# Chunk 1's attention output from channel-major products, with a repeated denominator divided on VectorE

## The chip, the cores and the metric

The kernel runs on one NeuronCore of a Trainium2 chip. The core has five engines with instruction streams of their own: TensorE (PE in the profile, with its weight loads as PEld), VectorE (DVE), ScalarE (ACT), GpSimd (POOL) and SyncE (SP, which issues most transfers). The metric is the device time of one execution in microseconds; lower is better.

## The reference

Two blocks follow one another. Everything is float32 at the kernel's inputs but `w_in`, `w_out`, `S1` and `S2`, which arrive as float64 and are rounded to float32 on the chip.

```python
# attention: batch 4, heads 4, seq 1088, head_dim 32, r = 8 sketches
a, b = S1 @ x, S2 @ x              # per token, 8 values each
phi(x) = outer(a, b)               # 64 features per token and head
kv  = sum_s phi(k)[s,f] * v[s,d]   # 64 x 32 per head
z   = sum_s phi(k)[s,f]            # 64 per head
x   = (phi(q) @ kv) / (phi(q) @ z + 1e-6)      # numerators / denominator

# MLP: 4352 tokens, d_model 128, d_ff 2048
h = x @ w_in
out = (0.5 * h * (1 + erf(h / sqrt(2)))) @ w_out
```

## The kernel before

**Tiling.** 1024 of a batch's 1088 tokens are cut into two chunks of 512 tokens, so there are eight chunks (0 to 7), and one of the 64-token remainders. For the MLP a chunk needs x in the form [128 channels, 512 tokens]; the 128 channels are 4 heads by 32. `w_in` and `w_out` lie in five pieces of 256, 256, 512, 512 and 512 columns (or rows) of d_ff; they are numbered 0 to 4 here. A piece is 128 columns times fi, so that fi 0 and 1 lie in piece 0, fi 2 and 3 in piece 1, fi 4 to 7 in piece 2.

**The MLP's steps.** `hidden(n, fi)` (L734) multiplies x of chunk n with 128 columns of `w_in` into one of two PSUM banks (`h_ps`), and ScalarE takes the GELU of it (L747). With two banks, a `hidden` waits until the GELU of the one before the last has emptied its bank. `first_hidden(n, half)` (L749) is the product for fi = 0, issued by halves of 256 tokens. `project(n, fi)` (L914, in the profile L925) multiplies a GELU output with the rows of `w_out` at fi. This usual way serves fi 0 to 3 of chunk 0 and fi 0 to 7 of chunk 1. All later blocks of four fi go by a method with seven half-size products in place of eight: GpSimd forms `token_sums` of the GELU outputs (L783, in the profile L791 to L794), and `two_products` (L813, L826) issues the products in pairs, two 64-column tiles side by side. The sums of `w_out` that this needs, `channel_sums(i)` of piece i (L768, L778 to L781), are formed once, on GpSimd too.

**The main loop** (L1256) goes through steps t. Steps 0 to 3 are chunk 0 with fi 0 to 3, steps 4 to 11 chunk 1 with fi 0 to 7, then chunk 0 goes on with fi 4 to 15, and so on. In each step come `hidden`, then the extra work that `at(t, ...)` put there, then the products that are due. Two steps are written out by hand, t = 3 and t = 4 (L1272, L1286). At its end the kernel fixes the order of the text on each engine: no engine's instructions are reordered, so an instruction that waits holds up all that stand behind it on its engine.

**Rounding the weights.** Each piece, two 32-bit words per weight, takes a chain: two field extractions on VectorE (L283 `bits_e`, L288 `bits_a`), the low word (L270) and the exponent (L294 `bits_r`, which needs L283) on ScalarE, then mantissa (L302 `bits_m`), sign (L307) and product (L312). Pieces 0 and 1 are done ahead of step 4. Pieces 2 to 4 are the six `turns`, from `begin(turns[0])` in step 4 on, nearly one after the other on VectorE. ScalarE's part of `turns[0]` is issued in step 4 ahead of the GELU of chunk 1's first hidden product.

**Chunk 1's x before the change** (step 3). `numerators_by_token` (L678, L685) has TensorE multiply the query features (64 features of two heads on 128 partitions, `qp`) with `kz_apart`, which holds kv and z side by side, so that numerators and denominators come out as [token, head x 33]. `divide` (L691) adds 1e-6, takes the reciprocal and multiplies on VectorE (L696, L698, L700), and `turn_half` (L717, L721) transposes the result by halves on TensorE into [channel, token]; ScalarE copies one half out of PSUM (L722) and VectorE the other. In between stand the rounding of `w_out` piece 1, whose mantissa step is done by ScalarE and GpSimd (L299, L300), and `project(0, 0)` and `project(0, 1)`, the latter in two halves between the transposes.

**z for chunk 0 and 1.** `z_cols` holds batch 0's z, each value repeated over 2 x 32 columns. Before the change it is made at step 40 (L525) and used at one place, `turn_first_kv` (L528).

**After piece 4.** In steps 13 to 16 `key_turn_blocks(1, r)` transposes batch 1's keys on VectorE (L383) and `features_of_all(1)` has TensorE use them (L1043). GpSimd makes piece 4's `w_out` product (`multiply`, L1141), and then goes on with `channel_sums(2)` and the first `token_sums`.

Of the kernel before, what the change touches and what calls it, by code (L numbers as in the profile page):

```python
# [8 lines left out]
FP = mybir.dt.float32  # L9
U32 = mybir.dt.uint32  # L10
AX = mybir.AluOpType
# [5 lines left out]
def kernel(  # L17
# [18 lines left out]
    pe, dve, act, pool, sp = nc.tensor, nc.vector, nc.scalar, nc.gpsimd, nc.sync  # L36
    B, H, S, D = q.shape
    R = S1.shape[0]
    F = R * R
# [3 lines left out]
    NP = H // 2  # L43
# [3 lines left out]
    JC = 4  # L47
    CW = JC * 128
    G = 128 // 32
    NCH = J // JC  # L50
    C = D + 1
# [9 lines left out]
    big = ctx.enter_context(tc.tile_pool(name="big", bufs=1))  # L61
    att = ctx.enter_context(tc.tile_pool(name="att", bufs=2))
# [9 lines left out]
    def work_bank():  # L72
        return work_banks()[:, 0]

    def halves(banks):
        return [banks[:, i] for i in range(2)]
# [437 lines left out]
        dve.tensor_mul(out=S_abc[b][:, :, :, 4:8], in0=c.rearrange("p (i f) -> p i f", i=2)[:, :, None].broadcast_to([128, 2, 2, 4]),  # L514
                       in1=own_r[:, None, :, None].broadcast_to([128, 2, 2, 4]))

    def repeat_first_z():

        to = kz_first.rearrange("f (c r d) -> f c r d", c=NP, r=2)
        for c in range(NP):  # L520
            act.copy(out=to[:F, c], in_=kz_apart[c * F:(c + 1) * F, :, c, 0:D])
        zs = att.tile([128, 2, D], FP, name="z_cols")
        for c in range(NP):
            rows = slice(c * F, (c + 1) * F)
            pool.tensor_copy(out=zs[rows], in_=kz_apart[rows, :, c, D:C].broadcast_to([F, 2, D]))  # L525
        held["zs"] = zs

    def turn_first_kv():  # L528

        ps, zs = work_bank(), held["zs"]  # L530
        for c in range(NP):
            pe.matmul(ps[c * F:(c + 1) * F, :F], lhsT=zs.rearrange("f r d -> f (r d)"), rhs=ident[:, c * F:(c + 1) * F],
                      start=True, stop=True)
        sketch_of_z(0, ps, 0)

# [128 lines left out]
    def take_x(n):  # L664

        W, banks, m = width[n], numerators_in.pop(n), 1 if n < NMAIN else B // 2
        xT[n] = att.tile([128, CW], FP, name="xT", bufs=3)
        to = xT[n][:, :W]
        to = to.rearrange("p (s x) -> p s x", s=2) if m == 1 else to.rearrange("p (s t i) -> p s i t", s=2, i=m)
        act.copy(out=to, in_=banks[:, :, :W // 2] if m == 1 else banks[:, :, :W // 2].rearrange("p s (i t) -> p s i t", i=m))  # L670

    x_tok = {}

# [4 lines left out]
    def numerators_by_token(n, banks, tokens):  # L678

        for at, i in enumerate(tokens):  # L680
            to = by_head(banks[at // 2]).rearrange("p (j c r) x -> p j r c x", j=2, c=NP)[:, at % 2]
            for r in range(2):
                for half in range(2):
                    rows, tok = slice(half * 64, (half + 1) * 64), i * 128 + half * 64
                    pe.matmul(to[rows, r], lhsT=qp[n][:, r, tok:tok + 64], rhs=kz_apart[:, r], start=True, stop=True)  # L685
# [5 lines left out]
    def divide(n, banks, first, den=None):  # L691

        if den is None:
            den = att.tile([128, NP, 2 * H], FP, name="den_tok")
            for i, bank in enumerate(banks):
                dve.tensor_scalar(out=den[:, i], in0=by_head(bank)[:, :, D], scalar1=1e-6, scalar2=None, op0=AX.add)  # L696
        den = den[:, :len(banks)]
        dve.reciprocal(out=den, in_=den)  # L698
        for i, bank in enumerate(banks):
            dve.tensor_mul(out=x_half(n, first + i).rearrange("p j h d -> p (j h) d"), in0=by_head(bank)[:, :, 0:D],  # L700
                           in1=den[:, i, :, None].broadcast_to([128, 2 * H, D]))
# [15 lines left out]
    def turn_half(n, i, ps, copy):  # L717
        if i == 0:
            xT[n] = att.tile([128, CW], FP, name="xT", bufs=3)
        for j in range(2):  # L720
            pe.transpose(ps[:, j * 128:(j + 1) * 128], in_=x_tok[n, i][:, j].rearrange("p h d -> p (h d)"), identity=ident)  # L721
        copy(out=xT[n][:, i * 256:(i + 1) * 256], in_=ps[:, :256])  # L722
# [26 lines left out]
    def first_hidden(n, half):  # L749

        if half == 0:
            first_banks[n, 0] = hidden_bank()
        parts = 1 if n else 2
        for i in range(parts):
            cols = slice(half * 256 + i * 256 // parts, half * 256 + (i + 1) * 256 // parts)
            pe.matmul(first_banks[n, 0][:, cols], lhsT=w_tile(w_in_sb, 0), rhs=xT[n][:, cols], start=True, stop=True)  # L756
# [157 lines left out]
    def project(n, fi, parts=range(B // 2), cols=slice(None)):  # L914
        first, final = fi == (BLOCKED if n == NMAIN else 0), fi == (USUAL[n] if n < NCH else NF) - 1
        if first and n not in o_of:
            o_of[n] = out_bank() if n < NMAIN else [out_bank() for i in range(B // 2)]
        g = g_of[n, fi]
        if n == NMAIN:

            for i in parts:
                pe.matmul(o_of[n][i][:, :128], lhsT=g[:, i * 128:(i + 1) * 128], rhs=w_tile(w_out_sb, fi),  # L922
                          start=first, stop=final)
            return
        pe.matmul(o_of[n][:, cols], lhsT=w_tile(w_out_sb, fi), rhs=g[:, cols], start=first, stop=final)  # L925
# [72 lines left out]
    for c in range(NP):  # L998
        rows = slice(c * F, (c + 1) * F)
        act.copy(out=kz_apart[rows, :, c], in_=kv_bank[rows, :128].rearrange("f (r x) -> f r x", r=2)[:, :, :C])  # L1000
    w_in[0].exponents()
    w_in[0].mantissas()
    by_act(**late.pop())
# [29 lines left out]
    def at(t, f, *a):  # L1033
        slots[t].append(lambda: f(*a))
# [40 lines left out]
    held = {}  # L1075
# [55 lines left out]
        for f in what:  # L1131
            getattr(rounding[w.name], f)()

    def end(w, product_by):
        r = rounding[w.name]
        r.mantissas()
        r.signs()
        if product_by is dve:
            r.product()

    def multiply(w):  # L1141
        rounding[w.name].product(pool)

    turns = [w[i] for i in range(2, 5) for w in (w_in_sb, w_out_sb)]
    both, low, exp = ("low_words", "exponents"), ("low_words",), ("exponents",)
# [1 line left out]
    for k, acts in enumerate(schedule):  # L1147
        t1 = acts[-1][0] if acts else 4
        if k + 1 < len(turns):
            at(t1, begin, turns[k + 1])  # L1150
        for t, what in acts:
            at(t, by_scalar, turns[k], *what)
        at(t1, end, turns[k], dve if k < 5 else pool)
    at(12, widen_v_rem, 1)
    at(13, multiply, turns[5])
    for i, t in enumerate((5, 6, 14)):
        at(t, channel_sums, i)
    at(16, channel_sums, 3)
    for r in range(2):
# [14 lines left out]
    at(26, lambda: turn_kv(1, held["kv"]))  # L1174
    at(24, query_outer, 2)
    at(6, spread_sketches)
    at(40, repeat_first_z)
    for n in range(3, NCHUNK):

        t = (n - 1) * NF  # L1180
# [75 lines left out]
    for t in range(len(steps) + LAG):  # L1256
        if t < 4:

            hidden(0, t)
            if t == 0:  # L1260
                expand_multiply(1, 0)
                w_out[0].fields()
                expand_copy(1, 1)
                expand_multiply(1, 1)
            if t == 1:
                w_out[0].low_words()
                w_out[0].exponents()
                w_out[0].finish()
                w_out[1].fields()
            if t == 2:  # L1270
                w_out[1].low_words()
            if t == 3:  # L1272
                banks = work_banks()
                numerators_by_token(1, halves(banks), range(JC))
                w_out[1].mantissas(by_pool=True)
                w_out[1].exponents()
                divide(1, halves(banks), 0)
                w_out[1].signs()
                w_out[1].product()
                project(0, 0)  # L1280
                project(0, 1, cols=slice(0, 256))
                turn_half(1, 0, work_bank(), by_act)
                project(0, 1, cols=slice(256, 512))
                turn_half(1, 1, work_bank(), by_dve)
            continue
        if t == 4:  # L1286
            begin(turns[0])
            by_scalar(turns[0], *both)
            first_hidden(1, 0)
            for f, *a in products[t]:  # L1290
                f(*a)
            first_hidden(1, 1)
        for n in drains[t]:
            drain(n)
        sooner = t == NMAIN * NF
        if sooner:
            for f, *a in products[t]:
                f(*a)
        if t < len(steps):
            n, fi = steps[t]  # L1300
            hidden(n, fi, by_halves=t >= 18)
        if t < len(steps) and steps[t][0] < NMAIN and steps[t][1] % NB == NB - 1:
            n, b = steps[t][0], steps[t][1] // NB
            if b >= first_block(n):
                token_sums(n, b)
        for f in slots[t]:
            f()
        for n in done[t]:
            store(n)
        if t != 4 and not sooner:  # L1310
            for f, *a in products[t]:
                f(*a)
    for n in done[len(steps) + LAG]:
# [40 lines left out]
```

## Time and profile before

| | us |
|---|---|
| median of 3 runs | 258.32 (257.75 to 258.34) |
| the profiled execution, its own time | 257.65 |
| its span | 255.9 |
| TensorE busy | 251.8 (98%) |
| VectorE busy | 156.9 (61%) |
| ScalarE busy | 114.6 (45%) |
| GpSimd busy | 177.6 (69%) |

A float32 product appears as two records on TensorE, one per pass: 512 columns through the whole array take 0.43 us each, 256 columns 0.215 us. The duration of a record contains the way through the array; what counts for the throughput is the distance from one start to the next. In a row of the timeline, "x4" joins four records, and the second number is the time from the first start to the last end. An instruction on VectorE, ScalarE or GpSimd that follows another without a wait starts a little before the other's recorded end.

### The profile page before, as it was taken

How to read it: one execution, taken by the hardware profiler on the slowest of the kernel's cores; microseconds unless marked ns; L12 is line 12 of the kernel's file. 1: busy time of each engine (PE TensorE's matmuls, PEld its weight loads, DVE VectorE, ACT ScalarE, POOL GpSimd, SP SyncE). 2: the span in 40 equal slices, each digit the busy share in tenths (PEclk: the TensorE clock that was granted, in tenths of full speed). 3: DMA queues.
4: the chain of work that ended last, by engine and by line, in shares of the span. 5: the costliest groups of instructions: out<-in, count | busy, mean ns of one | idle time of the engine just before them, and what ended most of it. 6: DMA issues, size and time to landing. Idle time of an engine off the chain costs nothing.

```text
span 255.9 us, 5994 instructions
## 1 busy us (share of the span) xinstructions
PE 251.8 (98%) x2427; PEld 132.7 (52%) x2427; DVE 156.9 (61%) x331; ACT 114.6 (45%) x221; POOL 177.6 (69%) x194
## 2 busy tenths in 40 slices
PE   8999999999999999999999999999999999999995
PEld 4755444555454546454444455445544444445784
DVE  4899995929798996570278976399507000700382
ACT  3785885323535334533335332623444334433541
POOL 3419329998849776687758874787758777877950
PEclk9999999999999999999999999999999999999999
DMA  6689657810001101111000011000110200020021
GB/s 210 205 267 295 168 116 195 222 31 10 0 3 18 23 4 23 20 19 25 3 0 0 0 17 29 1 4 0 27 16 7 36 1 3 5 36 3 0 35 31
DMA packets 29083, 13.50 MB, mean 53 GB/s; under 512 B 21888, under 2 KB 27264, under 8 KB 29056
## 3 DMA queue, kind: packets, MB, share of 16 engines
q1 hardware_dynamic: 28624, 12.79, 20.5%
q8 instruction: 19, 0.31, 0.5%
q10 hardware_dynamic: 432, 0.33, 0.4%
q14 instruction: 8, 0.07, 0.1%
HBM read 10.88 MB, written 2.23 MB: 51 GB/s over the span
## 4 chain that ended last, share of the span: by engine, by line
PE 98%; ACT 0%; DVE 0%; issue 0%
PE h_ps L740 45%; PE o_ps L826 35%; PE o_ps L925 4%; PE w_ps L896 2%; PE w_ps L456 1%; PE w_ps L604 1%; PE w_ps L659 1%; PE w_ps L957 1%; PE w_ps L570 1%; PE o_ps L922 1%; PE h_ps L756 1%; PE o_ps L445 1%; PE w_ps L1043 1%; PE h_ps L348 1%; PE w_ps L685 0%; PE o_ps L397 0%
## 5 line engine op out<-in xcount | busy, mean ns | idle before, releaser
L740 PE MATMUL h_ps<-xT,w_in 128*64 128x512 f32 (+2 forms) x536 | 138.0, 567 | 0.0
L747 ACT ACTIVATE block<-h_ps 128x512 f32<-128x512 f32 (+1 forms) x132 | 75.4, 572 | 119.5 <-PE h_ps L740 117.6
L826 PE MATMUL o_ps<-block,w_out 128*64 128x256 f32 x232 | 59.5, 379 | 0.0
L791 POOL TENSOR_TENSOR bits_low<-block 128x512 f32<-128x512 f32 x29 | 37.2, 1281 | 28.4 <-ACT block L747 28.4
L740 PEld LDWEIGHTS h_ps<-xT,w_in 128*64 128x64 f32 (+1 forms) x536 | 41.4, 140 | 26.9 <-issue 8.4
L826 PEld LDWEIGHTS o_ps<-block,w_out 128*64 128x64 f32 x232 | 31.7, 137 | 38.6 <-issue 27.4
L792 POOL TENSOR_TENSOR bits_a<-block 128x512 f32<-128x512 f32 x29 | 37.0, 1276 | 12.6 <-ACT block L747 12.6
L841 DVE COPY sums<-o_ps 64x256 f32<-64x256 f32 x8 | 3.3, 417 | 58.9 <-PE o_ps L826 58.9
L793 POOL TENSOR_TENSOR bits_e<-bits_a,block 128x512 f32<-128x512 f32 x29 | 37.3, 1288 | 2.3
L794 POOL TENSOR_TENSOR bits_m<-block,bits_e 128x512 f32<-128x512 f32 x29 | 37.1, 1279 | 2.3
L826 PE MATMUL o_ps<-bits_low,small 128*64 128x256 f32 x116 | 29.9, 380 | 0.0
L826 PE MATMUL o_ps<-block,small 128*64 128x256 f32 x116 | 29.9, 380 | 0.0
L826 PE MATMUL o_ps<-bits_a,small 128*64 128x256 f32 x116 | 29.8, 379 | 0.0
L826 PE MATMUL o_ps<-bits_m,w_out 128*64 128x256 f32 x116 | 29.8, 379 | 0.0
L826 PEld LDWEIGHTS o_ps<-block,small 128*64 128x64 f32 x116 | 15.6, 137 | 18.6 <-issue 11.2
L826 PE MATMUL o_ps<-bits_e,small 128*64 128x256 f32 x116 | 17.7, 383 | 0.0
L826 PEld LDWEIGHTS o_ps<-bits_a,small 128*64 128x64 f32 x116 | 15.8, 137 | 0.5 <-POOL bits_a L792 0.3
L826 PEld LDWEIGHTS o_ps<-bits_m,w_out 128*64 128x64 f32 x116 | 15.9, 137 | 0.0
L826 PEld LDWEIGHTS o_ps<-bits_low,small 128*64 128x64 f32 x116 | 15.6, 137 | 0.4 <-POOL bits_low L791 0.2
L616 DVE STREAM_TRANSPOSE w_ps<-w_ps 128x512 f32<-128x512 f32 (+1 forms) x7 | 4.8, 687 | 17.1 <-ACT xT L670 12.7
L826 PEld LDWEIGHTS o_ps<-bits_e,small 128*64 128x64 f32 x116 | 7.8, 137 | 11.5 <-issue 9.1
L925 PE MATMUL o_ps<-g,w_out 128*128 128x512 f32 (+1 forms) x26 | 12.4, 563 | 0.0
(223 smaller groups left out, 317.8 us busy)
## 6 DMA issues: line engine op xcount, KB each, us to landing
block<-in_moe_w_in_dram SPq DMA_DIRECT2D x3, 512.0 KB, 9.6
block<-in_moe_w_out_dram SPq DMA_DIRECT2D x3, 512.0 KB, 11.6
k<-in_k_dram SPq DMA_DIRECT2D x12, 128.0 KB, 3.2
v<-in_v_dram SPq DMA_DIRECT2D x12, 128.0 KB, 3.2
q<-in_q_dram SPq DMA_DIRECT2D x24, 64.0 KB, 2.5
out_dram<-oT SPq DMA_DIRECT2D x21, 64.0 KB, 2.2
q_first<-in_q_dram SPq DMA_DIRECT2D x2, 256.0 KB, 3.9
v<-in_v_dram SPq DMA_DIRECT2D x2, 256.0 KB, 4.2
```

Of the source, the lines that this page charges most:

```text
L348: pe.transpose(ps[:, i * 128:(i + 1) * 128], in_=s, identity=ident)
L616: dve.transpose(out=tok, in_=ps[:, :, :H2])
L740: pe.matmul(ps[rows, :W], lhsT=w[:, rows], rhs=xT[n][:, :W], start=True, stop=True)
L747: act.activation(out=g_of[n, fi][:, :W], in_=ps[:, :W], func=ACT.Gelu)
L791: pool.tensor_sub(out=s[3], in0=a11, in1=a21)
L792: pool.tensor_add(out=s[1], in0=a21, in1=a22)
L793: pool.tensor_sub(out=s[2], in0=s[1], in1=a11)
L794: pool.tensor_sub(out=s[4], in0=a12, in1=s[2])
L826: pe.matmul(acc[n][bank][half * 64:(half + 1) * 64, col:col + HW], lhsT=fixed, rhs=moving, start=opens and e == 0 and name in "4715", stop ...
L841: dve.tensor_copy(out=N[lo, 0, one], in_=a0[lo, one])
L896: pe.matmul(acc[NMAIN][rows, COLS_REM[name]], lhsT=tokens[:, rows], rhs=fixed, start=k == 0 and name == ORDER_REM[0], stop=k == BLOCKED // ...
L925: pe.matmul(o_of[n][:, cols], lhsT=w_tile(w_out_sb, fi), rhs=g[:, cols], start=first, stop=final)
```

## The change

- Chunk 1's x is no longer formed by token. `ratio_products` issues 16 products in tiles of 64 rows by 32 columns with the query features as the moving side, 256 tokens each: the numerators of a head go to bank 0 as [channel, token], and the denominators, with `z_cols` as weights, to bank 1, repeated over 32 partitions.
- `ratio_turn` transposes bank 1 in blocks of 32 x 32 on VectorE. `ratio` picks one column of each block, adds 1e-6, takes the reciprocal of [128, 16], and for each half of the tokens transposes the spread reciprocals back and multiplies the numerators with them, straight into x.
- The four transposes on TensorE, the two copies out of PSUM and the numerators by token of chunk 1 go.
- `w_out` piece 1 is rounded on VectorE alone, between `ratio_turn` and `ratio`; the ScalarE and GpSimd instructions of its mantissa go.
- In step 3 `project(0, 0)` and `project(0, 1)` follow one another whole; in step 4 `project(0, 2)` and `project(0, 3)`, which belonged to step 5, stand ahead of both halves of `first_hidden(1, ...)`.
- `z_cols` is made on GpSimd right after `kz_apart`, not in step 40.
- Piece 4's `w_out` product moves from GpSimd in step 13 to VectorE in step 12. `channel_sums` runs as piece 1 in step 5, piece 0 in step 6, piece 2 in step 13 (before: 0 in 5, 1 in 6, 2 in 14).

```diff
+    z_cols = big.tile([128, 2, D], FP, name="z_cols")
+    def widen_first_z():
+        for c in range(NP):
+            rows = slice(c * F, (c + 1) * F)
+            pool.tensor_copy(out=z_cols[rows], in_=kz_apart[rows, :, c, D:C].broadcast_to([F, 2, D]))
...
+    def ratio_products(n, banks):
+        for s in range(2):
+            for c in range(NP):
+                rows = slice(c * F, (c + 1) * F)
+                for r in range(2):
+                    for i, (h, w) in enumerate(((2 * c + r, kz_apart[rows, r, c, :D]), (2 * (1 - c) + r, z_cols[rows, r]))):
+                        pe.matmul(banks[h * D:(h + 1) * D, i, s * HW:(s + 1) * HW], lhsT=w,
+                                  rhs=qp[n][rows, r, s * HW:(s + 1) * HW], start=True, stop=True)
+    def ratio_turn(banks):
+        turned = att.tile([128, 2 * CW], FP, name="q_f", bufs=1)
+        dve.transpose(out=turned[:, :CW], in_=banks[:, 1])
+        return turned
+    def ratio(n, banks, turned):
+        den = att.tile([128, NP, 2 * H], FP, name="den_tok").rearrange("p c k -> p (c k)")
+        first = turned[:, :CW].rearrange("p (k x) -> p k x", x=D)[:, :, 0]
+        for c in range(NP):
+            dve.tensor_scalar(out=den[c * F:(c + 1) * F], in0=first[(1 - c) * F:(2 - c) * F], scalar1=1e-6, scalar2=None, op0=AX.add)
+        dve.reciprocal(out=den, in_=den)
+        xT[n] = att.tile([128, CW], FP, name="xT", bufs=3)
+        for s in range(2):
+            wide = turned[:, CW + s * HW:CW + (s + 1) * HW]
+            dve.transpose(out=wide, in_=den[:, s * 8:(s + 1) * 8, None].broadcast_to([128, 8, D]))
+            dve.tensor_mul(out=xT[n][:, s * HW:(s + 1) * HW], in0=banks[:, 0, s * HW:(s + 1) * HW], in1=wide)
...
     # right after kz_apart is copied
+    widen_first_z()
...
-        at(t1, end, turns[k], dve if k < 5 else pool)
+        at(t1, end, turns[k])
     at(12, widen_v_rem, 1)
-    at(13, multiply, turns[5])
-    for i, t in enumerate((5, 6, 14)):
+    for i, t in ((1, 5), (0, 6), (2, 13)):
         at(t, channel_sums, i)
...
             if t == 3:
                 banks = work_banks()
-                numerators_by_token(1, halves(banks), range(JC))
-                w_out[1].mantissas(by_pool=True)
+                ratio_products(1, banks)
+                turned = ratio_turn(banks)
                 w_out[1].exponents()
-                divide(1, halves(banks), 0)
-                w_out[1].signs()
-                w_out[1].product()
+                w_out[1].finish()
+                ratio(1, banks, turned)
                 project(0, 0)
-                project(0, 1, cols=slice(0, 256))
-                turn_half(1, 0, work_bank(), by_act)
-                project(0, 1, cols=slice(256, 512))
-                turn_half(1, 1, work_bank(), by_dve)
+                project(0, 1)
             continue
         if t == 4:
             begin(turns[0])
             by_scalar(turns[0], *both)
-            first_hidden(1, 0)
-            for f, *a in products[t]:
+            for f, *a in products[t] + products[t + 1]:
                 f(*a)
-            first_hidden(1, 1)
+            for half in range(2):
+                first_hidden(1, half)
...
-        if t != 4 and not sooner:
+        if t not in (4, 5) and not sooner:
             for f, *a in products[t]:
                 f(*a)
```

More of the change, by code (lines that the diff above doesn't have):

```diff
@@ L515, in sketch_of_z, with repeat_first_kz @@
                        in1=own_r[:, None, :, None].broadcast_to([128, 2, 2, 4]))
-    def repeat_first_z():
+    z_cols = big.tile([128, 2, D], FP, name="z_cols")
[3 more added lines that the diff above has]
+            pool.tensor_copy(out=z_cols[rows], in_=kz_apart[rows, :, c, D:C].broadcast_to([F, 2, D]))
+    def repeat_first_kz():
         to = kz_first.rearrange("f (c r d) -> f c r d", c=NP, r=2)
@@ L521, in repeat_first_z, with turn_first_kv @@
             act.copy(out=to[:F, c], in_=kz_apart[c * F:(c + 1) * F, :, c, 0:D])
-        zs = att.tile([128, 2, D], FP, name="z_cols")
+    def turn_first_kv():
+        ps = work_bank()
         for c in range(NP):
[L524 to L532, printed above, removed]
+            pe.matmul(ps[c * F:(c + 1) * F, :F], lhsT=z_cols.rearrange("f r d -> f (r d)"), rhs=ident[:, c * F:(c + 1) * F],
                       start=True, stop=True)
@@ L1132, in by_scalar, with end @@
             getattr(rounding[w.name], f)()
[L1134 to L1142, printed above, removed]
+    def end(w):
+        rounding[w.name].finish()
     turns = [w[i] for i in range(2, 5) for w in (w_in_sb, w_out_sb)]
@@ L1176 @@
     at(6, spread_sketches)
-    at(40, repeat_first_z)
+    at(40, repeat_first_kz)
     for n in range(3, NCHUNK):
```

## The prediction

> **What bounds the kernel.** I read the head of the page and the chain of waits first.
>
> ```profile
> span 255.9 us, 5994 instructions
> PE 251.8 (98%) x2427; PEld 132.7 (52%) x2427; DVE 156.9 (61%) x331; ACT 114.6 (45%) x221; POOL 177.6 (69%) x194
> ...
> PE 98%; ACT 0%; DVE 0%; issue 0%
> ```
>
> TensorE carries the whole chain. A microsecond taken from it is won only if TensorE doesn't wait for another engine instead, so I read the timelines around chunk 1's x: first TensorE's.
>
> ```profile
> 17.71 1.16 PE L685 MATMUL w_ps<-kz_apart,q_pT 128*64 128x66 f32 x32
> 18.80 1.56 PE L925 MATMUL o_ps<-g,w_out 128*128 128x512 f32 x4
> 20.19 0.38 PE L721 MATMUL w_ps<-ident,x_tok 128*128 128x128 f32 x2
> ...
> 21.06 0.67 PE L756 MATMUL h_ps<-xT,w_in 128*128 128x256 f32 x2
> 21.57 1.02 PE L925 MATMUL o_ps<-g,w_out 128*128 128x512 f32 x2
> 22.43 0.59 PE L756 MATMUL h_ps<-xT,w_in 128*128 128x256 f32 x2
> 22.86 1.02 PE L740 MATMUL h_ps<-xT,w_in 128*128 128x512 f32 x2
> 23.72 1.02 PE L925 MATMUL o_ps<-g,w_out 128*128 128x512 f32 x2
> 24.58 0.59 PE L740 MATMUL h_ps<-xT,w_in 128*128 128x512 f32 x1
> ```
>
> The starts follow one another almost without a hole. The last row is hidden(1, 2), which needs the bank that the GELU of (1, 0) empties; I take its start as the finish line of this stage. Then VectorE and ScalarE there.
>
> ```profile
> 18.91 0.24 DVE L696 TENSOR_SCALAR den_tok<-w_ps 128x8 f32<-128x8 f32 x2 [0.20 <-PE w_ps L685]
> 20.67 0.43 DVE L312 TENSOR_TENSOR w_out<-bits_m,bits_e 128x256 f32<-128x256 f32 x1
> 21.60 0.42 DVE L283 TENSOR_SCALAR bits_e<-block 128x512 uint32<-128x512 uint32 x1
> ...
> 41.75 0.73 DVE L1051 STREAM_TRANSPOSE w_ps<-w_ps 128x512 f32<-128x512 f32 x1 [2.55 <-PE w_ps L1043]
> ```
>
> ```profile
> 22.11 0.72 ACT L294 ACTIVATE bits_r<-bits_e,below 128x512 uint32<-128x512 uint32 x1 [0.55 <-DVE bits_e L283]
> 23.06 0.60 ACT L747 ACTIVATE g<-h_ps 128x512 f32<-128x512 f32 x1 [0.22 <-PE h_ps L756]
> ```
>
> Here is a chain that is just hidden now: VectorE's L283 at 21.60 releases ScalarE's L294, and behind L294 on ScalarE stands the GELU of (1, 0), with only 0.22 us to spare. Last, GpSimd after piece 4, and TensorE where it uses GpSimd's sums.
>
> ```profile
> 37.47 1.33 POOL L312 TENSOR_TENSOR w_out<-bits_m,bits_e 128x512 f32<-128x512 f32 x1 [1.23 <-DVE bits_e L307]
> 40.52 1.28 POOL L791 TENSOR_TENSOR bits_low<-block 128x512 f32<-128x512 f32 x1
> 49.26 1.28 POOL L791 TENSOR_TENSOR bits_low<-block 128x512 f32<-128x512 f32 x1
> ```
>
> ```profile
> 50.22 0.59 PE L826 MATMUL o_ps<-block,small 128*64 128x256 f32 x2
> 50.59 0.43 PE L826 MATMUL o_ps<-bits_low,small 128*64 128x256 f32 x1
> ```
>
> GpSimd runs without a break from 37.47 to beyond 59, and at 50.22 TensorE issues two products alone, in half the array, because their partners' `bits_low` ends only at 50.54. That costs it about 0.2 us (one row of 0.215 us at half use, twice).
>
> **TensorE's own work.** Removed: L685, 17.71 to 18.80, 1.09 us; four transposes, two from 20.19 to 20.41 and two of the same size, 0.44 us; and 0.08 us in which the first half of 21.06 waited for x (its two passes start 0.29 apart, not 0.215). Added: 16 products of 256 columns in 64x32 tiles, 32 records. The same form:
>
> ```profile
> 66.77 0.66 PE L604 MATMUL w_ps<-qT,S_abc 64*32 64x256 f32 x16
> 67.22 0.64 PE L659 MATMUL w_ps<-q_pT,kz 64*32 64x256 f32 x16
> ```
>
> Sixteen records, eight products, take 0.43 to 0.45 us from group to group, so all eight tile places work at once. Two such groups with the change of form before and behind them (L1043 at 40.98: 0.24 to its second row, the next form 0.31 after the last start) bring project(0, 0) to 17.71 + 0.24 + 2 x 0.215 + 0.05 + 0.31 = 18.73, against 18.80: 0.06 us less. In sum TensorE has 0.06 + 0.44 + 0.08 = 0.58 us less to do. The finish line could move from 24.58 to 24.00 plus what is now waited for. (In the new order project(0, 3) comes earlier, but it is done before hidden(1, 2) either way.)
>
> **First new wait: w_out piece 1.** The rounding now stands behind `ratio_turn` on VectorE. The products' last record ends at 18.42 + 0.38 = 18.80; VectorE starts 0.1 later, as L1051 does after L1043: 18.90. The 128x512 transpose takes 0.73 (L1051) and lets the next start after about 0.66: 19.56. Mantissa 0.34, sign 0.47 to the dependent product, product 0.43 (this kernel's L302, L307, L312 at 17.07 to 18.29): done at 20.79. GpSimd did the mantissa before, beside it; that is 0.34 us moved onto this path. ScalarE's exponent (L294 at 19.07) loses its predecessor L299 and isn't late. TensorE starts a product 0.16 us after the instruction it waited for (GELU end 15.62, next use of the bank 15.78): project(0, 2) at 20.95. Without the wait it would start after project(0, 0) and (0, 1), 18.73 + 0.96 + 0.86 = 20.55. Wait: 0.40 us. Behind it stand project(0, 3) and chunk 1's halves: project(0, 3) ends at 20.95 + 2 x 0.86 = 22.67.
>
> **Second: x itself.** After 20.75: two additions 0.1 each (L696), reciprocal 0.19 behind and 0.29 long: the transpose at 21.40. Nothing here shows a transpose of a spread, stride-0 operand; the nearest are 128x256 from SBUF, 0.44 (L551), and 128x256 within PSUM, 0.47 (L616's smallest). A third less or a third more are my bounds, since blocks are fed at the same rate or, repeated, stall; I take 0.47 with its hand-over. The multiplication is L700's, 0.42 (0.34 to the next). First half: 21.40 + 0.47 + 0.42 = 22.29, in time for 22.67. Second: 22.21 + 0.47 + 0.42 = 23.10, plus 0.16 is 23.26, where TensorE would be at 22.67 + 0.43 = 23.10. Wait: 0.16 us. hidden(1, 1) begins at 23.69 and TensorE is ready for hidden(1, 2) at 24.55.
>
> **Third: the GELU behind ScalarE's exponent.** VectorE reaches L283 at 23.02 instead of 21.60. It takes 0.42 to 0.54 (as L283 and L288 do at 21.60 to 23.40, slower beside GpSimd). ScalarE's L294 follows 0.09 later; the GELU of (1, 0) 0.66 after that, 0.60 long: end 24.79 to 24.91; hidden(1, 2) 0.16 later, 24.95 to 25.07. I take 25.0. The finish line moves from 24.58 to 25.0: 0.42 us late. So the 0.58 us saved turns into 1.0 us of waits. Bounds: with transposes a third shorter and L283 at 0.42 the line is 24.6, with them a third longer 25.4.
>
> The Trainium skill has a rule for L283's two durations (SBUF — State Buffer, Who interferes with whom): a VectorE instruction in a two-port mode and a GpSimd instruction block one another for a whole instruction. The rows show 0.12 us of stretching beside GpSimd; a whole GpSimd instruction there (L779, 0.5) would put the line at about 25.4 at most. Nothing else hangs on this.
>
> **VectorE's later work.** It runs 1.42 us late from 23.0 on, gains about 0.13 where it waited for ScalarE (26.14 to 26.87), and takes 0.6 for piece 4's product. Keys: 37.31 + 1.9 = 39.2, two transposes 1.29: 40.5, and TensorE wants them at 40.98 plus 0.4. Hidden, with 0.7 us to spare; the 2.55 us idle before L1051 absorb the rest. Piece 2 of `w_in`, ready at 25.45, becomes 26.9; TensorE uses it at 28.01. `w_out` piece 2 moves to 29.8; first use 32.30. Pieces 3 and 4 have more room.
>
> **GpSimd and the queues.** The two z copies (0.24 each, L525) fall into GpSimd's idle 2.9 us before 12.86, after the memsets that gate `w_out`'s transfers, so no transfer moves; SP issues the same. `channel_sums` waits for piece 1 until 20.8 instead of starting at 19.92; GpSimd's later 8 us wait for a transfer covers this. Losing 1.33 us at 37.47 lets it start the sums when the GELUs allow, 40.0 instead of 40.52 relative to TensorE. `bits_low` is then ready 0.5 us earlier, and the 0.2 us at 50.22 goes.
>
> **Sum** on the profiled execution: 257.65 - 0.58 + 1.0 - 0.2 = 257.87. The median is 0.67 above it, so 258.5.
>
> **Rivals.**
> 1. *The two row halves take turns (slower).* In L604, L659 and L1043 each half of the rows writes a bank of its own; in the new products both halves write both banks, each to other partitions. No row shows that. If they exclude one another, four tiles work at a time and the 0.86 us become 1.72; VectorE starts 0.86 later and everything behind it too: 258.5 + 0.86 = 259.4. It decides from full exclusion of more than 0.6 us on. Against: no partition of a bank is written by both at once. The Trainium skill (TensorEngine Tiling (Array Packing), Gotcha 1: PSUM Pressure) says that different row tiles can't use the same bank at one time and leaves it to software. By that rule it's this rival or a mere ban without a price; no run here shows it. Chance 0.17.
> 2. *The cover holds (faster).* VectorE is quicker than its rows, project(0, 2) and the GELU come in time: 258.32 - 0.58 - 0.2 = 257.5. Against: 1.0 us must vanish from three chained waits. Chance 0.13.
> 3. *VectorE's delay reaches the keys.* If it loses 0.9 us more in the six turns beside GpSimd (L302 took 0.81 there, 0.69 alone), features_of_all waits: some 0.4 us more, 258.9. Chance 0.10.
>
> **How the numbers follow.** The forecast has 0.60. About 0.3%, 0.8 us, is what a measurement of this kernel can tell. The forecast lies within it even at its bounds (258.1 to 258.9); rival 1 is slower in nearly all, rival 2 at the edge, half faster, rival 3 a third slower. Faster 0.10, same 0.70, slower 0.20. The range leaves out the outer halves of rivals 1 and 2: 257.6 to 259.3.
>
> **What would show it.** Of the changed kernel: 32 records of the new products in about 0.9 us (rival 1: 1.7); a wait of TensorE for `w_out` before project(0, 2) and one for the GELU before hidden(1, 2); VectorE's L283 near 23.0; no lone products near 50. I'm wrong if the 32x32 transposes are cheaper than 0.4 us, or if TensorE's holes sum to less than half a microsecond.

## The result and the profile after

The changed kernel takes 260.38 us (median of 7 runs, 258.89 to 261.07), the kernel before 258.31 us beside it (257.75 to 258.40). The ratio is 1.0081, with a 95% interval of 1.0054 to 1.0108: 2.1 us slower, where 258.5 was forecast with 259.3 as the upper end. The times also spread over 2.2 us, those of before over 0.65.

The profiled execution of the changed kernel took 259.42 us (span 257.6). Lines in its profile are about 30 higher than those of before: L770 is L740, L955 is L925, L808 to L811 are `channel_sums`, L821 to L824 `token_sums`, L1074 the product with the keys. Head of the page and shares of the chain of waits:

```profile
span 257.6 us, 5987 instructions
...
PE 85%; DMA 7%; SPq 5%; ACT 1%; issue 1%; DVE 0%; POOL 0%
```

TensorE no longer carries the whole chain. Somewhere it waits long enough for the chain to leave it. TensorE's timeline there, chunk 1's stage first:

```profile
17.95 0.40 PE L681 MATMUL w_ps<-q_pT,kz_apart 64*32 64x256 f32 x1
...
18.67 0.38 PE L681 MATMUL w_ps<-q_pT,z_cols 64*32 64x256 f32 x1
18.98 1.98 PE L955 MATMUL o_ps<-g,w_out 128*128 128x512 f32 x4
21.12 1.95 PE L955 MATMUL o_ps<-g,w_out 128*128 128x512 f32 x4 [0.16 <-DVE w_out L312]
22.91 1.28 PE L786 MATMUL h_ps<-xT,w_in 128*128 128x256 f32 x4
24.03 2.29 PE L770 MATMUL h_ps<-xT,w_in 128*128 128x512 f32 x4
26.15 1.02 PE L955 MATMUL o_ps<-g,w_out 128*128 128x512 f32 x2
...
42.65 1.14 PE L1074 MATMUL w_ps<-kT,S_ab 64*32 64x256 f32 x16 [0.88 <-DVE kT L383]
43.71 0.33 PE L348 MATMUL w_ps<-ident,k_rem 128*128 128x128 f32 x1
```

The kernel before at the same three places:

```profile
25.43 1.02 PE L925 MATMUL o_ps<-g,w_out 128*128 128x512 f32 x2
...
40.98 0.66 PE L1043 MATMUL w_ps<-kT,S_ab 64*32 64x256 f32 x16
41.57 0.33 PE L348 MATMUL w_ps<-ident,k_rem 128*128 128x128 f32 x1
```

What the span gained can be read from starts. The stage's first product starts 0.24 us later (17.95 instead of 17.71), all of it from the first 17 us, where two profiles of one and the same kernel differ by more than that (e8 and e10: 18.39 and 17.71). From there to project(1, 0) it takes 26.15 - 17.95 = 8.20 us, before 25.43 - 17.71 = 7.72: 0.48 us more. From there to the product with the keys 16.50 instead of 15.55, and the product itself takes 1.06 to the next form instead of 0.59: 1.42 us more. The rest, to the end of the span, is 213.9 instead of 214.3: 0.44 us less. In sum 0.24 + 0.48 + 1.42 - 0.44 = 1.70 us, which is the whole difference of the spans. The large term is the wait for the keys, `kT`. VectorE's timeline, the changed kernel first, then the kernel before:

```profile
23.35 0.48 DVE L283 TENSOR_SCALAR bits_e<-block 128x512 uint32<-128x512 uint32 x1
...
37.33 2.02 DVE L302 SCALAR_TENSOR_TENSOR bits_m<-bits_a,bits_low 128x512 f32<-128x512 uint32 x1
39.27 0.94 DVE L307 SCALAR_TENSOR_TENSOR bits_e<-block,bits_r 128x512 uint32<-128x512 uint32 x1
40.24 1.64 DVE L312 TENSOR_TENSOR w_out<-bits_m,bits_e 128x512 f32<-128x512 f32 x1
41.80 1.29 DVE L383 STREAM_TRANSPOSE kT<-k 128x512 f32<-128x512 f32 x2
```

```profile
36.01 0.78 DVE L302 SCALAR_TENSOR_TENSOR bits_m<-bits_a,bits_low 128x512 f32<-128x512 uint32 x1
36.71 0.68 DVE L307 SCALAR_TENSOR_TENSOR bits_e<-block,bits_r 128x512 uint32<-128x512 uint32 x1
37.31 1.29 DVE L383 STREAM_TRANSPOSE kT<-k 128x512 f32<-128x512 f32 x2
```

The mantissa of `w_out` piece 4 takes 2.02 us, where each other piece of this size took about 0.7, its sign 0.94 and its product 1.64. There is no idle time between them; the instructions themselves are longer. And GpSimd at the same time:

```profile
37.14 0.41 POOL L366 COPY v_rem_aug<-v_rem 64x128 f32<-64x128 f32 x1 [9.33 <-DMA v_rem<-in_v_dram]
37.52 0.44 POOL L808 TENSOR_TENSOR small<-w_out 128x128 f32<-128x128 f32 x1
...
38.87 0.79 POOL L811 TENSOR_TENSOR small<-w_out,small 128x128 f32<-128x128 f32 x1
39.62 1.71 POOL L821 TENSOR_TENSOR bits_low<-block 128x512 f32<-128x512 f32 x1
41.29 1.72 POOL L822 TENSOR_TENSOR bits_a<-block 128x512 f32<-128x512 f32 x1
43.09 1.27 POOL L823 TENSOR_TENSOR bits_e<-bits_a,block 128x512 f32<-128x512 f32 x1
```

L821 and L822 take 1.27 us elsewhere, as L823 does here. L302 is drawn out over three of GpSimd's instructions, L811 grows from 0.44 to 0.79, L821 is drawn out beside L307 and L312, and L822 beside L312. VectorE's transposes from 41.80 on have their usual 1.29 for two, with GpSimd just as busy. (The chain of waits leads from L383 to a transfer of v; but L383 reads k and starts as L312 ends, and in e1 and e2 below it starts 2 to 3 us earlier, again just as the instruction ahead of it ends.)

The kernel before had a wait here that kept the two apart: the product of `w_out` piece 4 was GpSimd's, and it had to wait for VectorE's signs. Behind it stood channel_sums(2). When the product went to VectorE, the wait went with it, and GpSimd ran into VectorE's chain.

### The profile page after: what moved, and what is told of

It reads as the page before. It is cut to its first block, busy times and chain, and to the rows that moved or that the text cites. A ratio compares the mean times of both kernels' runs of the same rounds, so it can differ in the third digit from the quotient of the medians.

```text
span 257.6 us, 5987 instructions
## 1 busy us (share of the span) xinstructions
PE 252.3 (98%) x2421; PEld 131.3 (51%) x2421; DVE 160.2 (62%) x335; ACT 113.6 (44%) x219; POOL 176.1 (68%) x192
## 4 chain that ended last, share of the span: by engine, by line
PE 85%; DMA 7%; SPq 5%; ACT 1%; issue 1%; DVE 0%; POOL 0%
PE h_ps L770 40%; PE o_ps L856 34%; DMA block<-in_moe_w_out_dram 6%; PE w_ps L926 2%; SPq L125 2%; PE w_ps L456 1%; PE w_ps L606 1%; PE w_ps L661 1%; PE w_ps L987 1%; SPq L136 1%; DMA v<-in_v_dram 1%; PE w_ps L1074 1%; PE o_ps L952 1%; SPq L109 1%; SPq L181 1%
## 5 line engine op out<-in xcount | busy, mean ns | idle before, releaser
L770 PE MATMUL h_ps<-xT,w_in 128*64 128x512 f32 (+2 forms) x536 | 137.3, 568 | 0.1
L821 POOL TENSOR_TENSOR bits_low<-block 128x512 f32<-128x512 f32 x29 | 37.9, 1306 | 30.5 <-ACT block L777 30.5
L770 PEld LDWEIGHTS h_ps<-xT,w_in 128*64 128x64 f32 (+1 forms) x536 | 40.8, 140 | 27.4 <-issue 8.2
L856 PEld LDWEIGHTS o_ps<-block,w_out 128*64 128x64 f32 x232 | 31.7, 137 | 39.2 <-issue 28.3
L822 POOL TENSOR_TENSOR bits_a<-block 128x512 f32<-128x512 f32 x29 | 37.5, 1294 | 12.3 <-ACT block L777 12.2
L823 POOL TENSOR_TENSOR bits_e<-bits_a,block 128x512 f32<-128x512 f32 x29 | 37.3, 1287 | 2.3
L824 POOL TENSOR_TENSOR bits_m<-block,bits_e 128x512 f32<-128x512 f32 x29 | 37.3, 1286 | 2.3
L955 PE MATMUL o_ps<-g,w_out 128*128 128x512 f32 x24 | 12.1, 600 | 0.2 <-DVE w_out L312 0.2
```

The costliest lines, as they stand in the source:

```text
L770: pe.matmul(ps[rows, :W], lhsT=w[:, rows], rhs=xT[n][:, :W], start=True, stop=True)
L821: pool.tensor_sub(out=s[3], in0=a11, in1=a21)
L822: pool.tensor_add(out=s[1], in0=a21, in1=a22)
L823: pool.tensor_sub(out=s[2], in0=s[1], in1=a11)
L824: pool.tensor_sub(out=s[4], in0=a12, in1=s[2])
L856: pe.matmul(acc[n][bank][half * 64:(half + 1) * 64, col:col + HW], lhsT=fixed, rhs=moving, start=opens and e == 0 and name in "4715", stop ...
```

## The experiments

Theory: VectorE and GpSimd block one another in piece 4's chain, and this makes most of the 2.1 us. Rival: VectorE is merely late there, by chunk 1's ratio (1.4 us) and the added product (0.6 us). The ratios below are to the kernel before, run beside each on the same chip; its median was 258.02 beside e1 to e4, 258.17 beside e5 to e8 and 258.07 beside e9 and e10. So the runs are compared by their distance from it, which is 2.1 us for the changed kernel. Below, "piece 4" without a name is `w_out` piece 4, the last of the six turns.

### e1: piece 4's product back on GpSimd

```diff
     # `end` and `multiply` as in the kernel before
 ...
-        at(t1, end, turns[k])
+        at(t1, end, turns[k], dve if k < 5 else pool)
     at(12, widen_v_rem, 1)
+    at(13, multiply, turns[5])
```

> The changed kernel, with piece 4's w_out product given back to GpSimd in step 13, ahead of channel_sums(2). Theory (VectorE and GpSimd block one another in piece 4's chain: the changed kernel's L302 took 2.02 us at 37.33 where 0.69 is usual, and GpSimd ran channel_sums and token_sums beside it): GpSimd has to wait for VectorE's signs, so they do not meet; L302 and L307 take 0.7 each again, the keys are ready near 39.8, TensorE's 1.0 us hole before L1074 goes, and the time is 258.3 + 0.4 = 258.7, with little spread. Rival (VectorE is merely late, by 1.4 us from chunk 1's ratio and 0.6 from the product): only the 0.6 us comes back, the hole shrinks to about 0.5 us, 259.8.

Measured: 259.20 us, ratio 1.0047 (1.0029 to 1.0066). L302 and L307 take 0.68 each, VectorE is idle for 1.95 us until the keys' product has ended, and there is no hole before L1074. The distance from the kernel before fell from 2.1 to 1.2 us, not to the 0.4 of the expectation: GpSimd, which now waits for a VectorE that is 1.2 us late, starts its first `bits_low` at 41.66 (before: 40.52), and TensorE waits for a later `bits_low`:

```profile
51.73 0.43 PE L856 MATMUL o_ps<-bits_low,small 128*64 128x256 f32 x1 [0.36 <-POOL bits_low L821]
```

From the first product there (50.77) to the change of form behind it (55.31) it takes 4.54 us, 0.58 more than in the kernel before (50.22 to 54.18). The rival's hole did not appear.

### e2: all work where the change put it, but GpSimd held

```diff
     at(12, widen_v_rem, 1)
+    gate = big.tile([128, 1], FP, name="gate")
+    at(13, lambda: pool.tensor_copy(out=gate, in_=w_out_sb[4][:, 0:1]))
```

> The changed kernel with all its work on the same engines, but one tiny GpSimd copy that reads piece 4's rounded w_out stands ahead of channel_sums(2), so that GpSimd waits until VectorE is through piece 4. Theory of mutual blocking: L302, L307 and L312 of piece 4 take 0.69 each, the keys are ready near 40.5, no hole before L1074; GpSimd's sums start near 39.3 instead of 37.5, which may cost 0.2 to 0.4 us later: 258.8 to 259.1. Rival (VectorE merely late): the hole stays at 1 us and the time at 260.4 or above.

Measured: 258.75 us, ratio 1.0031 (1.0019 to 1.0043). VectorE, GpSimd and TensorE there:

```profile
37.94 0.68 DVE L302 SCALAR_TENSOR_TENSOR bits_m<-bits_a,bits_low 128x512 f32<-128x512 uint32 x1
38.54 0.68 DVE L307 SCALAR_TENSOR_TENSOR bits_e<-block,bits_r 128x512 uint32<-128x512 uint32 x1
39.26 0.69 DVE L312 TENSOR_TENSOR w_out<-bits_m,bits_e 128x512 f32<-128x512 f32 x1
39.87 1.30 DVE L383 STREAM_TRANSPOSE kT<-k 128x512 f32<-128x512 f32 x2
```

```profile
40.01 0.19 POOL L1180 COPY gate<-w_out 128x1 f32<-128x1 f32 x1 [5.14 <-DVE w_out L312]
```

```profile
42.17 0.66 PE L1074 MATMUL w_ps<-kT,S_ab 64*32 64x256 f32 x16
```

This decides it. VectorE has the same instructions to do and is just as late from chunk 1, but from L302 to the keys it needs 1.93 us instead of 4.47, and TensorE has no hole. One copy of 0.19 us more on GpSimd brings the distance from the kernel before down from 2.1 to 0.7 us. The 2.5 us that VectorE lost were lost to GpSimd.

### e3: only piece 4's product moved, in the kernel before

```diff
-        at(t1, end, turns[k], dve if k < 5 else pool)
+        at(t1, end, turns[k], dve)
-    at(13, multiply, turns[5])
```

> The kernel before with only piece 4's w_out product moved to VectorE. Theory of mutual blocking: L302 at 36.0 meets channel_sums(2), which starts when v_rem has landed near 36, and takes well over 0.69 us (up to 2); but VectorE is 1.4 us earlier here and the keys have 2.4 us of cover, so the time stays within 0.3 us of before: 258.1 to 258.5. Rival (GpSimd not involved): L302 0.7 us as in the profile of before, and the same time.

Measured: 258.02 us, ratio 0.9996 (0.9981 to 1.0011). The remnants of v landed late in this profile, GpSimd began `channel_sums` at 37.41, and it was L312, not L302, that met it:

```profile
37.32 1.91 DVE L312 TENSOR_TENSOR w_out<-bits_m,bits_e 128x512 f32<-128x512 f32 x1
39.15 1.29 DVE L383 STREAM_TRANSPOSE kT<-k 128x512 f32<-128x512 f32 x2
```

So the blocking is there without the ratio form. In this execution it is paid out of VectorE's idle time before the keys: TensorE's product with the keys starts at 40.96, as before. But this is the fastest of ten times, which go from 257.29 to 258.67. TensorE has no lone products near 50 here, and in e8 that alone gave 0.44 us; yet the median is that of the kernel before. So the other executions may well lose something, perhaps where `v_rem` lands earlier and GpSimd meets more of the chain; no profile of one was taken. That the product alone costs nothing isn't shown.

### e4: a second profile of the changed kernel

> The changed kernel unaltered, a second profile of it. Its seven times spread from 258.89 to 261.07, those of before from 257.75 to 258.40. Theory: the spread comes from how long VectorE is blocked in piece 4, so this profile shows another duration of L302, L307 and L312 there, and its time moves with the hole before L1074: 0 to 2.5 us of hole for 258.7 to 261. Rival: the same hole at another time, or a hole elsewhere.

Measured: 260.69 us, one run, span 258.8. VectorE, then TensorE:

```profile
35.57 2.02 DVE L302 SCALAR_TENSOR_TENSOR bits_m<-bits_a,bits_low 128x512 f32<-128x512 uint32 x1
37.51 0.94 DVE L307 SCALAR_TENSOR_TENSOR bits_e<-block,bits_r 128x512 uint32<-128x512 uint32 x1
...
39.70 1.76 DVE L307 SCALAR_TENSOR_TENSOR bits_e<-block,bits_r 128x512 uint32<-128x512 uint32 x1
41.49 1.63 DVE L312 TENSOR_TENSOR w_out<-bits_m,bits_e 128x512 f32<-128x512 f32 x1
43.05 1.29 DVE L383 STREAM_TRANSPOSE kT<-k 128x512 f32<-128x512 f32 x2
```

```profile
43.89 1.14 PE L1074 MATMUL w_ps<-kT,S_ab 64*32 64x256 f32 x16 [2.10 <-DVE kT L383]
```

Here `v_rem` had landed by 35.38 instead of 37.14, GpSimd started sooner, and it met the chain of `w_in` piece 4, the turn before, as well. The hole before L1074 is 2.10 us by this row instead of 0.88, 1.2 more, and the time is 1.3 us more. That accounts for the difference of these two executions; that the whole spread of the changed kernel comes about so is likely, but two profiles don't show it. `v_rem` was copied at 33.6 to 37.3 in the profiles of the changed kernel and its variants, at 34.9 to 37.2 in those of the kernel before, and why it lands so unevenly stays open.

### e5: the sums of piece 4 later on GpSimd

```diff
     # on top of e2
-    at(18, channel_sums, 4)
+    at(19, channel_sums, 4)
```

> The kernel of e2 (the changed one with GpSimd held until piece 4 is through), with channel_sums(4) moved from step 18 to step 19, behind the second token_sums. Theory: e2's 0.36 us of TensorE waiting for bits_low near 51.7 came from GpSimd starting late, so that it goes, and only chunk 1's stage is left: 258.0 + 0.42 = 258.4. Rival (the wait near 51.7 is not GpSimd's order): 258.75 as e2.

Measured: 258.20 us, ratio 1.0002 (0.9993 to 1.0011). The wait near 51.7 is gone. From the first product there to the change of form it takes 3.55 us instead of 4.17 in e2, and the distance from the kernel before fell by 0.7 us (0.36 was expected). The kernel before has a loss of its own at this place, so e8 shows what e5 is to be compared with.

### e6: ScalarE's exponent behind the GELU

```diff
     # on top of e5, step 4
-            by_scalar(turns[0], *both)
+            by_scalar(turns[0], *low)
 ...
             hidden(n, fi, by_halves=t >= 18)
+        if t == 4:
+            by_scalar(turns[0], *exp)
```

> The kernel of e5, with ScalarE's exponent of turns[0] (L294) issued behind the GELU of chunk 1's first hidden product instead of ahead of it. Theory (third wait of the prediction): the GELU starts when its product is done, near 23.9 instead of 24.5, TensorE's hole of 0.3 + 0.1 us before hidden(1, 2) goes; 0.4 us less than e5: 258.0. Rival (the hole before hidden(1, 2) is TensorE's own change of order): no change against e5.

Measured: 257.86 us, ratio 0.9991 (0.9982 to 1.0000). TensorE in e5 (first) and e6, hidden(1, 1) and (1, 2) up to project(1, 0):

```profile
24.53 2.29 PE L770 MATMUL h_ps<-xT,w_in 128*128 128x512 f32 x4
26.66 1.02 PE L955 MATMUL o_ps<-g,w_out 128*128 128x512 f32 x2
```

```profile
24.39 1.98 PE L770 MATMUL h_ps<-xT,w_in 128*128 128x512 f32 x4
26.21 1.02 PE L955 MATMUL o_ps<-g,w_out 128*128 128x512 f32 x2
```

2.13 us become 1.82, and the median falls by 0.34. The GELU did wait behind the exponent.

### e7: the mantissa of piece 1 beside `ratio_turn`

```diff
     # on top of e6, step 3
+                w_out[1].mantissas(by_pool=True)
                 w_out[1].exponents()
-                w_out[1].finish()
+                w_out[1].signs()
+                w_out[1].product()
```

> The kernel of e6, with the mantissa of w_out piece 1 done by ScalarE and GpSimd beside ratio_turn, as before the change. Theory (first wait): project(0, 2) starts 0.3 us earlier, and VectorE's whole later work too; TensorE's 0.32 us hole before project(0, 2) nearly goes: 257.7, below the kernel before. Rival: the hole only moves on to chunk 1's halves, which wait for x: 258.0 as e6.

Measured: 258.22 us, ratio 1.0008 (0.9999 to 1.0017), slower than e6. GpSimd, VectorE and TensorE:

```profile
19.30 0.74 POOL L300 TENSOR_TENSOR bits_m<-bits_high,bits_low 128x256 f32<-128x256 f32 x1 [5.59 <-ACT bits_high L299]
```

```profile
19.66 0.66 DVE L307 SCALAR_TENSOR_TENSOR bits_e<-small,bits_r 128x256 uint32<-128x256 uint32 x1
20.84 0.43 DVE L312 TENSOR_TENSOR w_out<-bits_m,bits_e 128x256 f32<-128x256 f32 x1 [0.53 <-DVE bits_e L307]
```

```profile
21.42 1.95 PE L955 MATMUL o_ps<-g,w_out 128*128 128x512 f32 x4 [0.65 <-DVE w_out L312]
```

The same thing again, smaller: L307 meets GpSimd's L300 and takes 0.66 instead of 0.42. L312 starts 0.52 us after L307's end, where it followed 0.10 after it in the kernel before; what it waited for the rows don't show, as L300 had ended at 20.04. In the kernel before, the same L300 ran beside VectorE's L698 and L700, which take one operand from SBUF (L700's other one is in PSUM), and L307 came after it at its usual 0.42. Moving the mantissa to another engine saved VectorE an instruction of 0.38 us, but from the start of `ratio_turn` to that of the product it took 0.49 us longer than in e6 (1.88 instead of 1.39).

### e8 and e10: the kernel before with the later sums

```diff
     # on the kernel before
-    at(18, channel_sums, 4)
+    at(19, channel_sums, 4)
```

> The kernel before with channel_sums(4) in step 19 instead of step 18 and nothing else. Theory: the 0.2 us that TensorE lost at 50.22 to lone products goes; 257.8. It is the fair partner of e7. Rival: within 0.1 us of before, as e3, where this hole went too and the median did not move.

> The kernel of e8 once more, beside e9 on one chip: 257.7, 0.4 us below the kernel before. If e9's theory holds the two are within 0.1 us of one another, so that the channel-major form of chunk 1's x brings nothing over the form by token even with its waits mostly gone.

Measured: 257.73 us, ratio 0.9983 (0.9972 to 0.9994), and once more 257.58, ratio 0.9979 (0.9969 to 0.9989). The lone products of 50.22 are in pairs now:

```profile
50.91 0.38 PE L826 MATMUL o_ps<-block,small 128*64 128x256 f32 x1
50.92 0.38 PE L826 MATMUL o_ps<-bits_low,small 128*64 128x256 f32 x1
```

This one line is the only edit here whose interval lies clear of the kernel before on the faster side. It is worth 0.4 to 0.5 us, not 0.2. The loss doesn't stand at 50.22 itself: from there to the last `hidden` before the change of form it takes 2.59 us in the kernel before (52.81) and 2.58 here (53.49). It stands behind that, where the two column halves are out of step and one of them runs alone: 1.37 us to the change of form (54.18), here 0.96 (54.45). e5 is the changed kernel's form against this one: 258.20 to 257.73, 0.47 us slower, which is chunk 1's stage (8.20 us by the starts, here 7.73).

### e9: the mantissa of piece 1 ahead of `ratio_turn`

```diff
     # on top of e6, step 3
+                w_out[1].mantissas()
                 turned = ratio_turn(banks)
                 w_out[1].exponents()
-                w_out[1].finish()
+                w_out[1].signs()
+                w_out[1].product()
```

> The kernel of e6 with VectorE's mantissa of w_out piece 1 (L302, 0.34 us) ahead of ratio_turn, where VectorE waits about 0.2 us for the products, instead of behind it. Theory (first wait: VectorE's chain from ratio_turn to the product of piece 1 is what TensorE waits for, and in e7 GpSimd and VectorE's L307 blocked one another): ratio_turn starts 0.15 us later, all behind it 0.2 us earlier, the hole before project(0, 2) falls from 0.32 to about 0.13 us, and the time is 0.2 us below e6: 257.7, beside e10's 257.7. Rival: 257.9 as e6, the 0.2 us being lost again at x or at the GELU.

Measured: 257.71 us, ratio 0.9992 (0.9982 to 1.0001): no difference from e6, whose ratio is 0.9991. VectorE:

```profile
18.76 0.30 DVE L288 TENSOR_SCALAR bits_a<-small 128x256 uint32<-128x256 uint32 x1
19.16 0.42 DVE L302 SCALAR_TENSOR_TENSOR bits_m<-bits_a,bits_low 128x256 f32<-128x256 uint32 x1
19.51 0.71 DVE L686 STREAM_TRANSPOSE q_f<-w_ps 128x512 f32<-128x512 f32 x1
```

The mantissa needs L288's result and can only start after it has ended, so it doesn't fit into the gap; `ratio_turn` starts 0.26 us after it could, not 0.15. Of the hole before project(0, 2) 0.09 us went. Beside e10 it stays 0.13 us behind by the medians and 0.3 by the ratios, whose intervals overlap; by the starts its stage takes 7.80 us and e10's 7.72. With its waits mostly removed, the channel-major form comes close to the form by token and isn't ahead of it.

## Why the prediction was wrong

**What failed: "VectorE's later work" and "GpSimd and the queues".** The first counted 0.6 us for piece 4's product and found the keys hidden "with 0.7 us to spare"; the second counted only the gain from GpSimd "losing 1.33 us at 37.47". Each is right for its engine alone: with GpSimd held (e2), the keys' transposes start at 39.87 in a profile whose stage starts 0.71 late, where 39.2 was forecast, and the keys are hidden. Together they let GpSimd work beside three VectorE instructions that read two operands from SBUF, and those took 4.47 us instead of 1.93 (e2). The row that would have told was among those shown: GpSimd's L312 at 37.47 with 1.23 us of idle time, ended by VectorE's `bits_e`. I read it as time in which GpSimd is slow; it was also what held GpSimd off. The profile of before has what looks like the same effect, with GpSimd as the loser:

```profile
20.20 0.54 POOL L779 TENSOR_TENSOR small<-w_out 128x64 f32<-128x64 f32 x1
20.70 0.56 POOL L780 TENSOR_TENSOR small<-w_out,small 128x64 f32<-128x64 f32 x1
```

They ran beside VectorE's L307 (20.15) and L312 (20.67) of `w_out` piece 1, which kept their 0.42 and 0.43. In the changed kernel instructions of the same lines and size run beside the ratio (21.33 and 21.61) and take 0.32 each. None of the prediction's own signs of being wrong came: the 32x32 transposes took 0.43 to 0.45 us, and TensorE's holes came to over 2 us.

**Rival 3** had the place, VectorE's delay reaching the keys, but not the cause or the size: 0.4 us from 0.81 against 0.69 us in L302. The measured hole with its slower product was 1.4 us, in the second profile about 2.6.

**The rule of the Trainium skill** (SBUF — State Buffer, Who interferes with whom) was used for L283 only and then set aside with "nothing else hangs on this". What was missed hung on it. By that page a VectorE instruction with two SBUF inputs and a GpSimd instruction that reads SBUF exclude one another too. The runs agree as to which instructions suffer: L302, L307 and L312 do, the transposes don't. The size was beyond one GpSimd instruction: L302 lost 1.33 us, three of 0.44. That the cause is a shared port is the page's account; the runs show which instructions slow one another, and that keeping them apart ends it.

**What held.** *TensorE's work*: the 32 records start within 0.72 us and the next form 0.31 after the last, 1.03 in all as forecast; rival 1 (the row halves taking turns) would have shown 0.86 more. *First wait*: 0.40 forecast; project(0, 0) at 18.98 plus 0.96 and 0.86 is 20.80, and the product started at 21.12, 0.32 later, and its four records took 0.07 more than at full rate, so 0.39. *Second*: 0.16 forecast, 0.25 measured by the starts. *Third*: L283 forecast at 23.02, with the stage's 0.24 us shift 23.26, measured 23.35; the exponent and the GELU:

```profile
23.93 0.72 ACT L294 ACTIVATE bits_r<-bits_e,below 128x512 uint32<-128x512 uint32 x1 [4.03 <-DVE bits_e L283]
24.56 1.12 ACT L777 ACTIVATE g<-h_ps 128x512 f32<-128x512 f32 x2
```

TensorE's hole before hidden(1, 2) is 0.40, where 0.45 was forecast. The stage came out 0.48 us late, forecast 0.42, and e6 shows the third wait by taking most of it away. *GpSimd's gain*: there, but mis-sized, 0.41 us instead of 0.2, for the reason given at e8.

By the starts of each profile, three stretches account for the distances to within 0.2 us, but for two rows: chunk 1's stage (to project(1, 0)), the way from there to the form behind the keys' product, and the way from there to the change of form at 54.18. In us over the kernel before; the last column is between medians, beside the kernel before:

| | stage | keys | sums | together | measured |
|---|---|---|---|---|---|
| forecast | 0.42 | 0 | -0.2 | 0.2 | |
| changed kernel | 0.48 | 1.42 | -0.41 | 1.49 | 2.07 |
| e4, one run | 0.48 | 2.64 | -0.41 | 2.71 | 2.67 |
| e1 | 0.48 | 0 | 0.58 | 1.06 | 1.18 |
| e2 | 0.49 | 0 | 0.21 | 0.70 | 0.73 |
| e5 | 0.48 | 0 | -0.41 | 0.07 | 0.03 |
| e6 | 0.17 | 0 | -0.41 | -0.24 | -0.31 |
| e7 | 0.66 | 0 | -0.41 | 0.25 | 0.05 |
| e9 | 0.08 | 0 | -0.41 | -0.33 | -0.36 |
| e8 | 0.01 | 0 | -0.42 | -0.41 | -0.44 |
| e10 | 0 | 0 | -0.42 | -0.42 | -0.49 |
| e3 | 0.01 | 0 | -0.42 | -0.41 | 0.00 |

The keys are the term that the prediction put at nothing. The changed kernel's profile is of one of its faster executions (259.42, median 260.38), e3's of its fastest, so in these two rows the last column is well above the sum.

## What to carry to other kernels

An instruction that waits can be what keeps two engines out of each other's way. Before it is moved, one should see what stands behind it in its queue, at what time that will now run, and whether the two engines' instructions of that time are of kinds that slow one another, as VectorE's with two SBUF operands and GpSimd's sums did here. A few tenths of cover left on an engine are worth little when another part of the same change puts a neighbour beside it; the two parts have to be summed at the place where they meet.

## What was not expected of the hardware

- A VectorE instruction with two SBUF operands (128x512) took 0.94 to 2.02 us instead of 0.69 beside GpSimd's subtractions and additions (the changed kernel, e3 and e4), and GpSimd's 128x512 ones took 1.6 to 1.7 instead of 1.27. VectorE's 32x32 transposes kept their 0.65 us beside them.
- Two row halves of 64x32 tiles wrote the same two PSUM banks, on different partitions, at full speed: four groups of eight records at distances of 0.21 to 0.25 us.
- A 32x32 transpose of a spread operand with a stride of 0, 128x256, took 0.43 to 0.45 us, the same as 0.44 for a plain one.
